# Local-head attention in units of 32 queries and 64 keys, with one transpose, copy and normalisation per 256 tokens

## The chip, the cores and the metric

One core of a Trainium2 chip. The time of a kernel is the device time of one execution in microseconds (us); several runs are made and their median is given. Beside it there is one profiled execution, from which every row below comes.

## The reference

Attention over 4 batches, 8 heads, 576 positions and 64 channels, then two feed-forward layers over the 2304 tokens with 512 channels. The first four heads look at the last 32 positions only, and these are the heads that the change touches:

```python
rel = pos[:, None] - pos[None, :]
mask_local = (rel >= 0) & (rel < 32)                      # heads 0 to 3
mask_strided = (rel >= 0) & (pos[None, :] % 32 == pos[:, None] % 32)   # heads 4 to 7
scores = np.where(masks, q @ k.T / sqrt(64), -1e9)
attn = exp(scores - max); attn = attn / (attn.sum(-1) + 1e-9)
x = attn @ v                      # -> (2304, 512)
h = x @ w_in; x = (h - tanh(h)) @ w_out                   # 512 -> 2048 -> 512
xn = x / rms(x) * rms_g
out = (silu(xn @ w_gate) * (xn @ w_val)) @ w_out2         # 512 -> 1536 -> 512
```

## The kernel before

The 2304 tokens are cut into nine subs of 256 tokens (`subs`): 0 to 3 are the first 256 positions of each batch, 4 is the last 64 positions of all four batches, 5 to 8 are positions 256 to 511. A sub has a `Local` object for heads 0 to 3 and, for heads 4 to 7, a `Dense` one (subs 0 to 3 and 6, on TensorE) or a `Strided` one (on GpSimd and VectorE). The subs form five groups, and while TensorE computes the first feed-forward layer of one group (`pe_h`, tiles ps_h; `pe_x`, tiles ps_x), the attention of the next group is put between. `Work` holds that attention as a list of stages, in the order local s, local p, dense s, local v, dense p, dense v; `run_pe` takes the next one at the steps that `STINT` names. From the second group on TensorE's order is the order in which the program is written. The order on the other engines is set by a scheduler at build time.

A stage of the local heads is one of three. **s** (`st_s`): 16 matmuls of a 64x64 block of q against 96 keys for the 256 queries, into two PSUM banks; then VectorE adds the mask and takes the maxima (`st_m`, one instruction per head and half), ScalarE takes the exponentials with their sums (`st_e`), VectorE divides (`st_n`, three instructions per half of 128 queries). **p** (`st_p`, `st_c`): per half four transposes and one copy of 96 partitions. **v** (`st_v`): 16 matmuls of a 96x64 block of v against 64 queries, then `st_y` (ScalarE) and `st_z` (VectorE) write the high and the low part into xs. `load_qk` and `load_v` of the next sub are issued behind s and v. The flag `fused` makes one p and one copy serve both halves; before, only `Dense` of subs 0 to 3 has it.

The attention of subs 0 and 1 has nothing to hide behind. Its order is written out as words in the string `START`, for all engines at once (`first` reads it): s, m, e, n, p, c, v, y, z as above, with the number of the sub, L (local) or D (dense) and the half; A, B, P, Q decode a weight tile in four steps (scale on ScalarE L170, merge on VectorE L176 and L177, high part on ScalarE L184, low part on VectorE L188); h, T, G, I, J, X are the pieces of the feed-forward units that come first (matmul into ps_h, tanh, subtract, high, low, matmul into ps_x). The line after `<` is the order of the loads, all on SyncE's queue. In subs 0 and 1 (`early`) the mask is added by TensorE (ps_s<-tab) and the maximum is a plain reduction. Matmuls all have line 147 (`mm`), transposes line 437.

Of the kernel before, what the change touches and what calls it, by code (L numbers as in the profile page):

```python
# [25 lines left out]
W9 s0Lx m0L0 e0L0 m0L1 s0Dx n0L0 e0L1 m0D0 p0L0m1 m0D1 s1Lx A0 e0D0 B0 c0L0a n0L1 p0L1h1 P0 Q0 m1L0 m1L1 e0D1 c0L1a  # L26
v0Lh0 s1Dx n0D1 n0D0 A1 e1L0 p0Dh1 e1L1 y0L1 n1L0 m1D0 m1D1 c0Da n1L1 v0Dm0m1 y0L0 e1D0 y0D1 z0L0 y0D0 z0L1 p1L0h1
c1L0a B1 z0D0 P1 z0D1 p1L1h1 e1D1 c1L1a Q1 n1D0 n1D1 h0h0 A2 v1Lm1 T0 B2 A3 G0 y1L0 p1Dh1 c1Da y1L1 B3 v1Dh1m0 I0 P2
J0 y1D1 z1L0 y1D0 h1h0 T1 z1L1 z1D1 z1D0 P3 h2h1 Q2 G1 A4 Q3 T2 B4 I1 G2 J1 I2 J2 X0
# [4 lines left out]
def attn_moe_moe_kernel(  # L34
# [3 lines left out]
    near_v: bass.AP,  # L38
# [4 lines left out]
    v_loc: bass.AP,  # L43
# [74 lines left out]
    tab = one.tile([128, 544], F32, name="tab")  # L118
    ident, mask, dmask = tab[:, 192:320], tab[:, 320:416], tab[:, 416:544]
    add = tab[:, 0:192].bitcast(BF16)  # L120
    ident16, add = add[:, 0:128], {96: add[:, 128:320].rearrange("q (u t) -> q u t", u=2), 64: add[:, 320:384]}
# [228 lines left out]
    class Heads:  # L350
        def __init__(self, j):
            self.j, self.near, self.early = j, j < NEAR, j < EA
            self.ps, self.sm, self.nm, self.ss, self.pp, self.pT, self.v = {}, {}, {}, {}, {}, {}, {}
            self.slot, self.both, self.sums = {}, None, None
            self.fused = False
# [9 lines left out]
        size = {"sm": 512, "pT": 512, "v": 512}  # L365

        def st_s(self, bank):
# [3 lines left out]
            for hh in range(2):  # L371
                if self.early:
                    m = add[w]
                    m = m.unsqueeze(2) if w == 96 else m.unsqueeze(1).unsqueeze(1)
# [12 lines left out]
        def st_m(self, i):  # L387
# [10 lines left out]
            self.ss[i] = att.tile([128, 2, 2], F32, tag="ss", name="ss", bufs=4)  # L398
            m = dmask if w == 128 else mask if not self.near else add[96][:, i] if w == 96 else add[64]
# [22 lines left out]
        def st_n(self, i):  # L422
            sm, ss = self.sm[i], self.ss.pop(i)
# [3 lines left out]
                out=sm, in0=sm, in1=ss.unsqueeze(3).to_broadcast([128, 2, 2, self.w]), op=ALU.mult  # L427
# [27 lines left out]
    class Local(Heads):  # L455
        w = 96

        def __init__(self, j):
            super().__init__(j)
            self.runs = runs(j)  # L460
            self.at, self.kw = [], 0
            if self.near:
                self.at, self.kw = [0, 32, 96, 160], SUB
            else:
                for _, _, n, _ in self.runs:
                    self.at += range(self.kw, self.kw + n, 64)
                    self.kw += W + n

        def load_qk(self):
# [6 lines left out]
            for b, t0, n, x0 in self.runs:  # L476
# [4 lines left out]
                o = self.at[x0 // 64]  # L481
                nc.sync.dma_start(out=self.kT[:, :, o:o + W + n], in_=k_loc[b, :, :, t0 - W:t0 + n])

        def load_v(self, i):
            if self.early:
                t = held.tile([128, 1024], F32, tag="v", name="v")[0:96]
                nc.sync.dma_start(out=t, in_=near_v[self.j])
                for i in range(2):
                    self.v[i] = t[:, 512 * i:512 * i + 512].rearrange("k (u f) -> k u f", u=2)
                return  # L490
            t = self.room("v", i, 512)[0:96]
            self.v[i] = t.rearrange("k (u f) -> k u f", u=2)
            if self.near:
                nc.sync.dma_start(out=t, in_=near_v[self.j, :, 512 * i:512 * i + 512])
                return
            at = [b * S + t - W for b, t in subs[self.j][2 * i:2 * i + 2]]
            first = v_loc[0, 0:96, :]
            (sp, _), (sf, nf) = first.ap
            nc.sync.dma_start(
                out=self.v[i],  # L500
                in_=bass.AP(
                    tensor=first.tensor, offset=v_loc.offset + at[0] * sp,
                    ap=[[sp, 96], [(at[1] - at[0]) * sp, 2], [sf, nf]],
                ),
            )

        def st_v(self, bank):
            ps = bank("ps_v").rearrange("r (i p u t) -> r i p u t", i=2, u=2, p=2)
            for i in range(2):
# [9 lines left out]
            self.po = {i: ps[:, i] for i in range(2)}  # L519
# [202 lines left out]
    class Work:  # L722
# [23 lines left out]
        def stage(o, nm):  # L746
            if nm == "s":
# [4 lines left out]
                for i in range(2):  # L752
# [10 lines left out]
            if nxt:  # L763
                if nm == "s":
                    nxt.load_qk()
                if nm == "v" and isinstance(o, Local):
                    for i in range(2):
# [671 lines left out]
```

## Time and profile before

| | |
|---|---|
| median of 3 runs | 889.43 us (888.55 to 890.35) |
| the profiled execution | 887.7 us |
| its span, first to last instruction | 885.9 us (so 1.8 us lie around it) |
| mean granted TensorE clock | 0.996 |
| TensorE (PE) busy | 868.8 us, 98% |
| VectorE (DVE) busy | 668.5 us, 75% |
| ScalarE (ACT) busy | 397.9 us, 45% |
| GpSimd (POOL) busy | 280.0 us, 32% |

Matmuls overlap in the array and the ends of the records are modelled, so the price of a group of matmuls is read from its start to the start of the group behind it. A float32 matmul leaves two records.

### The profile page before, as it was taken

The numbers are of one execution on the slowest core, as the hardware profiler recorded it, in microseconds if no ns is written. First come the engines' busy times: TensorE is split into PE (matmuls) and PEld (weight loads), VectorE is DVE, ScalarE is ACT, GpSimd is POOL, SyncE is SP. The second block draws the span as 40 slices with busy tenths as digits, with TensorE's granted clock in tenths as the row PEclk, the third lists the DMA queues.
The fourth block names the chain that finished last, engine by engine and source line by source line (L and its number), as shares of the span: only waits on it lengthen the run. The fifth ranks groups of instructions, "written<-read, shape, count | busy, mean of one in ns | idle before, by whom it ended". The sixth has DMA issues, their size and how long they took to land.

```text
span 885.9 us, 14105 instructions
## 1 busy us (share of the span) xinstructions
PE 868.8 (98%) x5091; PEld 739.7 (83%) x5091; DVE 668.5 (75%) x1376; ACT 397.9 (45%) x897; POOL 280.0 (32%) x315
## 2 busy tenths in 40 slices
PE   6999999999999999999999999999999999999998
PEld 4888888888998887888887888888878988888986
DVE  5999788888779887179978898576997953445444
ACT  6987643332544333265637553355332533422320
POOL 0000147695276952000000569676442400000000
PEclk8999999999999999999999999999999999999999
DMA  9955224311313000199828777799659139955002
GB/s 328 379 196 173 77 73 151 111 50 36 116 54 110 28 16 1 46 291 346 280 72 270 279 250 270 252 415 364 232 179 349 48 114 355 397 168 166 1 0 84
DMA packets 58566, 157.84 MB, mean 178 GB/s; under 512 B 9536, under 2 KB 20672, under 8 KB 58496
## 3 DMA queue, kind: packets, MB, share of 16 engines
q1 hardware_dynamic: 57344, 155.89, 50.0%
q10 hardware_dynamic: 1152, 1.05, 0.3%
q8 instruction: 40, 0.66, 0.3%
q14 instruction: 30, 0.25, 0.1%
HBM read 119.16 MB, written 37.75 MB: 177 GB/s over the span
## 4 chain that ended last, share of the span: by engine, by line
PE 82%; DVE 8%; POOL 5%; ACT 2%; issue 1%; DMA 1%; SPq 0%; DVEq 0%; POOLq 0%; ACTq 0%
PE ps_x L147 21%; PE ps_h L147 21%; PE ps_pr L147 18%; PE ps_o L147 12%; POOL pr L629 4%; PE ps_m L147 4%; PE ps_q L147 3%; DVE so L669 3%; DMA raw<-in_w_in_dram 1%; PE ps_s L147 1%; POOL pr L662 1%; PE ps_v L147 1%; ACT sm L416 1%; PE ps_p L437 1%; DVE x L957 0%
## 5 line engine op out<-in xcount | busy, mean ns | idle before, releaser
L147 PE MATMUL ps_h<-xs,w 128*128 128x512 f32 (+1 forms) x984 | 213.4, 365 | 0.7 <-DVE tg L814 0.7
L147 PE MATMUL ps_x<-g,w 128*128 128x512 f32 (+1 forms) x984 | 214.0, 366 | 0.0
L147 PEld LDWEIGHTS ps_h<-xs,w 128*128 128x128 f32 x984 | 169.0, 189 | 30.6 <-DVE tg L814 1.1
L147 PEld LDWEIGHTS ps_x<-g,w 128*128 128x128 f32 x984 | 168.6, 189 | 30.0 <-issue 0.2
L147 PE MATMUL ps_pr<-xt,wt 128*128 128x448 f32 x576 | 123.1, 366 | 2.2 <-DVE s L1040 1.4
L629 POOL TENSOR_TENSOR pr<-sk,sq 128x256 f32<-128x256 f32 (+2 forms) x101 | 82.5, 852 | 131.8 <-DMA sq<-in_q_str_dram 126.4
L147 PE MATMUL ps_o<-wt,p 128*128 128x512 f32 x504 | 120.2, 390 | 0.0
L147 PEld LDWEIGHTS ps_pr<-xt,wt 128*128 128x128 f32 x576 | 107.9, 188 | 13.5 <-DVE s L1040 2.2
L147 PEld LDWEIGHTS ps_o<-wt,p 128*128 128x128 f32 x504 | 94.6, 188 | 18.7
L820 ACT CAST g<-tg 128x512 fp32r<-128x512 f32 (+1 forms) x82 | 46.6, 568 | 108.9 <-DVE tg L814 108.8
L662 POOL TENSOR_TENSOR pr<-sv,se 128x288 f32<-128x288 f32 (+12 forms) x104 | 69.7, 691 | 56.7 <-DVE so L669 19.8
L1050 ACT COPY u<-ps_pr 128x448 f32<-128x448 f32 x72 | 38.2, 533 | 84.8 <-PE ps_pr L147 84.7
L814 DVE SCALAR_TENSOR_TENSOR tg<-ps_h,tg 128x512 f32<-128x512 f32 (+1 forms) x82 | 50.8, 619 | 28.0 <-ACT tg L809 28.0
L669 DVE TENSOR_REDUCE so<-pr 128x16 f32<-128x272 f32 (+11 forms) x104 | 65.0, 653 | 8.7 <-POOL pr L662 8.4
L971 POOL TENSOR_TENSOR tr<-x 128x896 f32<-128x896 f32 x4 | 15.1, 3765 | 171.1 <-DMA raw<-in_w_gate_dram 153.9
L809 ACT ACTIVATE tg<-ps_h 128x512 f32<-128x512 f32 (+1 forms) x82 | 44.2, 539 | 48.1 <-PE ps_h L147 48.1
L1101 DVE SCALAR_TENSOR_TENSOR osum<-ps_o,osum 128x512 f32<-128x512 f32 x70 | 47.9, 687 | 21.6 <-PE ps_o L147 20.9
L825 DVE TENSOR_TENSOR g<-tg,g 128x512 fp32r<-128x512 f32 (+1 forms) x82 | 55.3, 677 | 10.8 <-ACT g L820 10.2
L147 PE MATMUL ps_pr<-xt,wo 128*128 128x448 f32 x288 | 60.8, 366 | 0.2 <-ACT u L1050 0.2
L147 PEld LDWEIGHTS ps_pr<-xt,wo 128*128 128x128 f32 x288 | 54.0, 188 | 5.2 <-ACT u L1050 0.6
L184 ACT CAST w<-ct 128x512 fp32r<-128x512 f32 x68 | 42.1, 619 | 30.3 <-DVE ct L177 28.2
L634 DVE TENSOR_REDUCE sc<-pr 128x4 f32<-128x256 f32 (+2 forms) x101 | 43.8, 437 | 12.1 <-POOL pr L629 11.6
(110 smaller groups left out, 1201.4 us busy)
## 6 DMA issues: line engine op xcount, KB each, us to landing
wt<-w SPq DMA_DIRECT2D x84, 512.0 KB, 5.9
raw<-in_w_out_dram SPq DMA_DIRECT2D x28, 512.0 KB, 6.1
raw<-in_w_gate_dram SPq DMA_DIRECT2D x24, 512.0 KB, 5.9
raw<-in_w_val_dram SPq DMA_DIRECT2D x24, 512.0 KB, 6.8
w<-w SPq DMA_DIRECT2D x24, 512.0 KB, 6.6
w<-wo SPq DMA_DIRECT2D x24, 512.0 KB, 8.2
raw<-in_w_in_dram SPq DMA_DIRECT2D x16, 512.0 KB, 9.9
out_dram<-osum SPq DMA_DIRECT2D x18, 256.0 KB, 2.1
```

What stands on the lines that cost most here:

```text
L147: nc.tensor.matmul(out_, lhsT, rhs, start=start, stop=stop, skip_group_check=True)
L184: nc.scalar.copy(out=self.t[:, 0].rearrange("p c f -> p (c f)"), in_=self.b)
L629: nc.gpsimd.tensor_tensor(out=pr, in0=self.k[:, a:e, :], in1=self.q[:, c - c0:c - c0 + 1, :].to_broadcast([128, e - a, D]), op=ALU.mult,)
L634: pend.append(lambda: nc.vector.tensor_reduce(out=s[:, c - c0, a:e], in_=pr, axis=AX.X, op=ALU.add))
L662: nc.gpsimd.tensor_tensor(out=pr, in0=self.v[:, 0:c + 1, a:e], in1=self.e[:, c - c0, 0:c + 1].unsqueeze(2).to_broadcast([128, c + 1, e - a ...
L669: pend.append(lambda: nc.vector.tensor_reduce(out=o[:, c - g0, a:e], in_=pr.rearrange("l c d -> l d c"), axis=AX.X, op=ALU.add))
L809: nc.scalar.activation(out=t, in_=h_of[g, f, a], func=ACTF.Tanh, scale=WS)
L814: nc.vector.scalar_tensor_tensor(out=t, in0=h_of.pop((g, f, a)), scalar=WS, in1=t, op0=ALU.mult, op1=ALU.subtract)
L820: nc.scalar.copy(out=t[:, 0], in_=t_of[g, f, a])
L825: nc.vector.tensor_tensor(out=t[:, 1], in0=t_of.pop((g, f, a)), in1=t[:, 0].bitcast(F32), op=ALU.subtract)
L1050: nc.scalar.copy(out=u, in_=x[kd])
L1101: nc.vector.scalar_tensor_tensor(out=o, in0=ps, scalar=WS, in1=o, op0=ALU.mult, op1=ALU.add)
```

## The change

`Local` now works on units of 32 queries, each with the 64 keys that end with its own: its key offsets `at` are 32 apart, `w` is 64 and `fused` is on. So s has 32 matmuls of a 64x32 block of q against 64 keys; the probabilities of both halves lie side by side, 128 columns wide, and n, p and c are one each for 256 queries (p: four transposes of 128x128, c: a copy of 128 partitions). For v the 64 keys of the first half stand on partitions 0 to 63 and those of the second on 64 to 127: 32 matmuls of 64x64 against 32 queries, one half into one PSUM bank and the other into a second. v comes from a new input `v_win`, in which the windows lie ready as 128 rows of 1024 numbers for each sub (512 KB, in place of 96 rows, 384 KB), in one transfer where subs 2 to 8 had two. The mask table is 480 numbers wide instead of 544. `START` is a new list.

```diff
 START = """
 <tabcdwABwCDwww2ww
-W9 s0Lx m0L0 e0L0 m0L1 s0Dx n0L0 e0L1 m0D0 p0L0m1 m0D1 s1Lx A0 e0D0 B0 c0L0a n0L1 p0L1h1 P0 Q0 m1L0 m1L1 e0D1 c0L1a
+W9 s0Lx s0Dx m0L1 m0L0 e0L1 e0L0 m0D1 m0D0 e0D1 n0L p0Lm0 A0 s1Lx B0 e0D0 s1Dx c0La P0 m1L1 A1 v0Lh0h1 m1L0 e1L1 n0D
...
+            n = self.unit
             for i in range(2):
                 for p in range(2):
-                    for k in range(2):
+                    for x in range(0, 128, n):
                         for hh in range(2):
-                            r, u = slice(64 * hh, 64 * hh + 64), 2 * i + k
+                            r, t = slice(64 * hh, 64 * hh + 64), 128 * i + x
+                            a = self.at[t // n]
                             mm(
-                                ps[hh][64 * k:64 * k + 64, i, p, :], self.q[r, u, p, :],
-                                self.kT[r, p, self.at[u]:self.at[u] + w], not self.early, True,
+                                ps[hh][x:x + n, i, p, :], self.q[r, t // 64, p, t % 64:t % 64 + n],
+                                self.kT[r, p, a:a + w], not self.early, True,
                             )
...
     def st_n(self, i):
-            sm, ss = self.sm[i], self.ss.pop(i)
+            if self.fused:
+                sm = self.both.rearrange("q h p i t -> q (h p i) t")
+                ss = self.sums.rearrange("q h p i -> q (h p i)")
...
     class Local(Heads):
-        w = 96
+        w = 64
...
+            self.fused, self.local, self.unit = True, True, W
...
-        def load_v(self, i):
+        def load_v(self):
             if self.early:
...
+                t = held.tile([128, 1024], F32, tag="v", name="v")
+            else:
+                t = one.tile([128, 1024], F32, tag="v", name="v")
+            self.v = t.rearrange("k (c f) -> k c f", f=256)
+            nc.sync.dma_start(out=t, in_=v_win[self.j])
 
         def st_v(self, bank):
-            ps = bank("ps_v").rearrange("r (i p u t) -> r i p u t", i=2, u=2, p=2)
-            for i in range(2):
-                pT, v = self.pT.pop(i), self.v.pop(i)
-                for u in range(2):
-                    for p in range(2):
-                        for hh in range(2):
-                            h = 2 * p + hh
+            ps = [bank("ps_v")[:, :256].rearrange("r (p t) -> r p t", p=2) for _ in range(2)]
+            pT = self.pT.pop(0)
+            for c in range(4):
+                for p in range(2):
+                    for hh in range(2):
+                        for i in range(2):
+                            h, r, x = 2 * p + hh, slice(64 * i, 64 * i + 64), W * c
                             mm(
-                                ps[64 * hh:64 * hh + 64, i, p, u, :], v[:, u, 64 * h:64 * h + 64],
-                                pT[:, hh, p, 64 * u:64 * u + 64], True, True,
+                                ps[i][64 * hh:64 * hh + 64, p, x:x + W], self.v[r, c, 64 * h:64 * h + 64],
+                                pT[r, hh, p, x:x + W], True, True,
                             )
```

What that does to the order is seen at two places. The first is TensorE from the transposes of sub 1's local heads to the first ps_x of the feed-forward layer (v<-pT,v are the local values, pT,dv the dense ones, ps_h the feed-forward units, ps_s<-lq the scores of sub 2). Before:

```order
L437 MATMUL ps_p<-tab,sm 96x128 x8
L147 MATMUL ps_h<-xs,w 128x256 x12
L147 MATMUL ps_v<-pT,v 64x64 x16
L437 MATMUL ps_p<-tab,sm 128x128 x4
L147 MATMUL ps_v<-pT,dv 32x64 x32
L147 MATMUL ps_h<-xs,w 128x256 x12
L147 MATMUL ps_s<-lq 64x96 x13
L147 MATMUL ps_h<-xs,w 128x256 x12
L147 MATMUL ps_x<-g,w 128x256 x12
```

and now:

```order
L450 MATMUL ps_p<-tab,sm 128x128 x4
L146 MATMUL ps_h<-xs,w 128x256 x12
L146 MATMUL ps_v<-pT,v 64x32 x32
L450 MATMUL ps_p<-tab,sm 128x128 x4
L146 MATMUL ps_h<-xs,w 128x256 x12
L146 MATMUL ps_s<-lq 32x64 x8
L146 MATMUL ps_v<-pT,dv 32x64 x32
L146 MATMUL ps_x<-g,w 128x256 x12
L146 MATMUL ps_h<-xs,w 128x256 x6
```

The second ps_h unit has moved ahead of the dense values of sub 1, and the first ps_x ahead of the third ps_h unit. The second place is ScalarE, from the copy of sub 1's first local transposes to the copy that the dense values of sub 1 wait for (the last pT<-ps_p here; ca<-raw are scale steps, w<-ct casts of weight tiles). Before:

```order
L442 COPY pT<-ps_p 96x512
L184 CAST w<-ct 128x512
L416 ACTIVATE sm,ss<-ps_s,nm 128x64 x4
L442 COPY pT<-ps_p 96x512
L170 ACTIVATE ca<-raw 128x512
L809 ACTIVATE tg<-ps_h 128x256
L170 ACTIVATE ca<-raw 128x512
L445 CAST xs<-ps_v 128x2x128
L442 COPY pT<-ps_p 128x512
```

and now, from the exponentials of sub 1's dense heads on:

```order
L424 ACTIVATE sm,ss<-ps_s,nm 128x64 x8
L455 COPY pT<-ps_p 128x512
L183 CAST w<-ct 128x512
L805 ACTIVATE tg<-ps_h 128x256
L183 CAST w<-ct 128x512
L458 CAST xs<-ps_v 128x2x128 x2
L816 CAST g<-tg 128x256
L455 COPY pT<-ps_p 128x512
```

A second weight cast, a second evacuation and the cast of g now stand ahead of the last copy, where they stood behind it. Of the two scale steps one (`A2` in the words) has moved up, ahead of the first of these rows, and the other (`A3`) behind the last; one local copy is gone.

## Rows read from the trace of the kernel before

**Rows 1.** Page, part 1: busy time of each engine, share, instructions

```profile
PE 868.8 (98%) x5091; PEld 739.7 (83%) x5091; DVE 668.5 (75%) x1376; ACT 397.9 (45%) x897; POOL 280.0 (32%) x315
```

**Rows 2.** Page, part 4: chain that ended last, share by engine

```profile
PE 82%; DVE 8%; POOL 5%; ACT 2%; issue 1%; DMA 1%; SPq 0%; DVEq 0%; POOLq 0%; ACTq 0%
```

**Rows 3.** Waits of TensorE: who waited for whom, total us, times, longest

```profile
PE ps_v L147 <- ACT pT L442: 1.8, 2, 1.2
...
PE ps_h L147 <- DVE tg L814: 0.7, 1, 0.7
```

**Rows 4.** Busy time by stretch (PE, PEld, DVE, ACT, POOL, clock, DMA share, GB/s)

```profile
10.00:20.00 10.00, 7.79 (x112) 5.94 (x112) 7.98 (x29) 8.66 (x45) 0.00 (x0) 0.66 1.03 363
20.00:30.00 10.00, 6.92 (x191) 6.01 (x192) 9.48 (x29) 9.99 (x36) 0.00 (x0) 1.00 1.04 345
30.00:40.00 10.00, 10.00 (x91) 8.86 (x90) 10.00 (x33) 8.11 (x20) 0.00 (x0) 1.00 1.03 407
```

**Rows 5.** Timeline of TensorE, sub 4's local stages: start, us, instruction, records

```profile
147.50 0.89 PE L147 MATMUL ps_s<-lq 64*64 64x96 f32 x32
148.32 3.06 PE L147 MATMUL ps_x<-g,w 128*128 128x512 f32 x12
...
159.39 1.04 PE L437 MATMUL ps_p<-tab,sm 128*96 128x128 f32 x8
160.18 3.00 PE L147 MATMUL ps_x<-g,w 128*128 128x512 f32 x12
...
171.26 1.15 PE L147 MATMUL ps_v<-pT,v 96*64 96x64 f32 x32
172.35 3.02 PE L147 MATMUL ps_x<-g,w 128*128 128x512 f32 x12
```

**Rows 6.** Timeline of TensorE, sub 3's dense stages s, p and v

```profile
102.16 0.69 PE L147 MATMUL ps_s<-dq 64*64 64x64 f32 x32
102.78 3.92 PE L147 MATMUL ps_x<-g,w 128*128 128x512 f32 x16
...
114.66 0.60 PE L437 MATMUL ps_p<-tab,sm 128*128 128x128 f32 x4
115.01 2.77 PE L147 MATMUL ps_h<-xs,w 128*128 128x512 f32 x11
...
120.20 0.86 PE L147 MATMUL ps_v<-pT,dv 64*32 64x64 f32 x64
120.99 0.50 PE L147 MATMUL ps_x<-g,w 128*128 128x512 f32 x1
```

**Rows 7.** Timeline of TensorE around the end of START

```profile
28.29 0.86 PE L147 MATMUL ps_v<-pT,dv 64*32 64x64 f32 x64 [0.68 <-ACT pT L442]
29.07 1.69 PE L147 MATMUL ps_h<-xs,w 128*128 128x256 f32 x12
30.70 1.10 PE L147 MATMUL ps_s<-lq 64*64 64x96 f32 x26
...
34.70 2.91 PE L147 MATMUL ps_h<-xs,w 128*128 128x512 f32 x12
```

**Rows 8.** Timeline of ScalarE in START

```profile
16.93 0.67 ACT L170 ACTIVATE ca<-raw 128x512 f32<-128x512 f32 x1 [0.79 <-DMA raw<-in_w_in_dram]
...
25.41 0.58 ACT L442 COPY pT<-ps_p 96x512 f32<-96x512 f32 x1
...
27.65 0.59 ACT L442 COPY pT<-ps_p 128x512 f32<-128x512 f32 x1
...
28.39 0.42 ACT L820 CAST g<-tg 128x256 fp32r<-128x256 f32 x1
28.70 0.63 ACT L184 CAST w<-ct 128x512 fp32r<-128x512 f32 x1
```

**Rows 9.** Groups by line and shape, VectorE: count, busy us, mean ns, idle before

```profile
L426 DVE TENSOR_TENSOR sm<-sm,ss 128x384 f32<-128x384 f32 x18 | 10.8, 598 | 0.2
...
L426 DVE TENSOR_TENSOR sm<-sm,ss 128x512 f32<-128x512 f32 x2 | 1.5, 746 | 0.0
```

More of the change, by code (lines that the diff above doesn't have):

```diff
@@ L42, in attn_moe_moe_kernel @@
     k_loc: bass.AP,
-    v_loc: bass.AP,
+    v_win: bass.AP,
     q_str: bass.AP,
@@ L354, in __init__ @@
             self.slot, self.both, self.sums = {}, None, None
-            self.fused = False
+            self.fused, self.local, self.unit = False, False, 64
         def room(self, name, i, words):
@@ L397, in st_m @@
             self.nm[i] = nm = att.tile([128, 2, 2], F32, tag="nm", name="nm", bufs=4)
-            self.ss[i] = att.tile([128, 2, 2], F32, tag="ss", name="ss", bufs=4)
-            m = dmask if w == 128 else mask if not self.near else add[96][:, i] if w == 96 else add[64]
+            if not self.fused:
+                self.ss[i] = att.tile([128, 2, 2], F32, tag="ss", name="ss", bufs=4)
+            else:
+                if self.sums is None:
+                    self.sums = att.tile([128, 2, 2, 2], F32, tag="ss", name="ss", bufs=4)
+                self.ss[i] = self.sums[:, :, :, i]
+            if self.local:
+                m = add_l[:, i] if self.near else mask
+            else:
+                m = add_d if self.near else dmask
             for hh in range(2):
@@ L426, in st_n @@
             nc.vector.tensor_tensor(
-                out=sm, in0=sm, in1=ss.unsqueeze(3).to_broadcast([128, 2, 2, self.w]), op=ALU.mult
+                out=sm, in0=sm, in1=ss.unsqueeze(2).to_broadcast(list(sm.shape)), op=ALU.mult
             )
@@ L480, in load_qk @@
                 )
-                o = self.at[x0 // 64]
+                o = self.at[x0 // W]
                 nc.sync.dma_start(out=self.kT[:, :, o:o + W + n], in_=k_loc[b, :, :, t0 - W:t0 + n])
-        def load_v(self, i):
+        def load_v(self):
             if self.early:
-                t = held.tile([128, 1024], F32, tag="v", name="v")[0:96]
-                nc.sync.dma_start(out=t, in_=near_v[self.j])
-                for i in range(2):
[L489 to L505, printed above, removed]
@@ L518, in st_v @@
                             )
-            self.po = {i: ps[:, i] for i in range(2)}
+            self.po = {i: ps[i].rearrange("r p (u t) -> r p u t", t=64) for i in range(2)}
         def dst(self, i):
@@ L751, in stage @@
                     o.st_e(i)
-                for i in range(2):
+                for i in range(1 if o.fused else 2):
                     o.st_n(i)
@@ L765, in stage @@
                     nxt.load_qk()
-                if nm == "v" and isinstance(o, Local):
-                    for i in range(2):
-                        nxt.load_v(i)
-                elif nm == "v":
+                if nm == "v":
                     nxt.load_v()
@@ L1375, in values @@
         return residues(v, n).transpose(0, 5, 3, 4, 1, 2, 6).reshape(B, 8 * n, 4, 4 * D)
-    row, col = _np.arange(128)[:, None], _np.arange(96)[None, :]
-    r2 = row % 64
-    rel = r2 + 32 - col
-    near = (rel >= 0) & (rel < 32)
-    first = _np.where(row < 64, (r2 >= col) & (r2 - col < 32), near)
-    c2 = _np.arange(64)[None, :]
+    row, c2 = _np.arange(128)[:, None], _np.arange(64)[None, :]
+    r1, r2 = row % 32, row % 64
+    near = (r1 + 32 >= c2) & (r1 < c2)
+    first = _np.where(row < 32, row >= c2, near)
     same = (r2 // 8 == c2 // 8) & (c2 <= r2)
@@ L1403, in lay_out, with windows @@
     v_l = v[:, :4].transpose(0, 2, 1, 3).reshape(B, S, 4 * D)
+    subs = [[(b, t + 64 * u) for u in range(4)] for t in (0, 256) for b in range(B)]
+    subs[B:B] = [[(b, 512) for b in range(B)]]
+    def windows(sub):
+        r = [v_l[b, max(0, t + x - 32):][:64] for b, t in sub for x in (0, 32)]
+        return _np.stack(r).reshape(2, 4, 64, 4 * D).transpose(0, 2, 1, 3).reshape(128, 1024)
     q_d = residues(q, 16).reshape(B, 2, 2, 2, 8, 4, 8, D).transpose(0, 3, 2, 7, 5, 1, 6, 4).reshape(B, 2, 128, 512)
@@ L1406, in lay_out @@
         near_l=flat(q_l[:, :, :8], k_l[:, :, :, :256]),
-        near_v=flat(*(v_l[:, a:a + 96] for a in (0, 32, 96, 160))),
         near_d=flat(q_d[:, 0], keys(8)), v_near=values(8).reshape(B, 64, 2, 2, 256).transpose(0, 2, 1, 3, 4).reshape(B, 128, 512),
-        q_loc=q_l, k_loc=k_l, v_loc=v_l,
+        q_loc=q_l, k_loc=k_l, v_win=_np.stack([windows(s) for s in subs]),
         q_str=lanes(q), k_str=lanes(k), v_str=lanes(v),
```

36 lines of the change are left out of this document (18 added, 18 removed).

## The prediction

> **What bounds the kernel now.** I read the page's busy times first: TensorE works 868.8 of 885.9 us, and no other engine over 75% [rows 1]. The chain of waits says the same from the other end: 82% of what ended last is TensorE [rows 2]. So a microsecond of TensorE time taken out of the dense part is a microsecond of the kernel, as long as nobody else becomes late, and work of VectorE or ScalarE counts only where TensorE stands. The waits say where that is: 1.8 us for the copy pT in front of the values, and once 0.7 us for VectorE's tg in front of a ps_h unit [rows 3]. The stretches show the first kind in START: from 20 to 30 us TensorE is busy 6.92 of 10 while ScalarE is at 9.99, and from 30 us on TensorE is full [rows 4]. In the stretch before, the granted clock is 0.66, a mixture of its two levels, 1.2 and 2.4 GHz, after TensorE had stood still between short bursts; it is back at 1.00 from 20 us on. There are therefore two terms: the price of the local stages on TensorE in subs 2 to 8, which lie in the dense part, and the length of ScalarE's queue in START, which holds subs 0 and 1.
>
> **The local stages of subs 2 to 8.** The price is taken from the start of a stage to the start of the matmuls behind it. Sub 4: scores 148.32 - 147.50 = 0.82 us, transposes 160.18 - 159.39 = 0.79, values 172.35 - 171.26 = 1.09, together 2.70 us [rows 5]. The other six subs repeat this to within 0.1.
>
> Scores now: 32 matmuls of a 64x32 block against 64 columns. The same shape is in the trace, as the dense values of sub 3: 32 matmuls (64 records) in 120.99 - 120.20 = 0.79 us [rows 6], 24.6 ns each. The old ones cost 51 ns each (0.82 / 16). So twice the count is paid by eight tiles of the array at work where there were four, and by 64 columns in place of 96: 0.79, a gain of 0.03.
>
> Transposes now: four of 128x128, as in the dense stage: 115.01 - 114.66 = 0.35 [rows 6]. A gain of 0.44.
>
> Values now: 32 matmuls of a 64x64 block against 32 columns. No row has that. The two rows with 64x64 blocks are 16 matmuls against 64 columns, 102.78 - 102.16 = 0.62 [rows 6], and against 96 columns, 0.82 [rows 5]; the line through them gives 0.42 at 32 columns, so 0.84 for 32 matmuls. The bounds: 0.79 below, the cheapest matmul of the trace, and 1.24 above, if a matmul against 32 columns costs as much as one against 64 (32 x 38.8 ns). I take 0.84, since the line rests on the same blocks and the cheapest matmul lies right beside it. A gain of 0.25, with bounds of a gain of 0.30 and a loss of 0.15.
>
> Against that stands a rule of the Trainium skill (TensorEngine Tiling (Array Packing), Instruction Overhead): each matmul carries about 60 cycles, so that one column costs as much as 60, and a tiling factor is not to be taken from a dimension that is small already. By it the values would be at the upper bound, 1.24, and the sum below 2.8 us smaller. The trace speaks half for it: the price per column between 64 and 96 is straight, but no row lies under 64 columns. It has a chance of its own among the rivals.
>
> Sum: 2.70 - (0.79 + 0.35 + 0.84) = 0.72 us for a sub, times seven = 5.0 us (bounds 2.2 and 5.4). All of it lies in the dense part and nothing hides it. The values now need two PSUM banks at once where one did, but the stage ahead of them always lies several feed-forward units back, so its banks are free.
>
> **VectorE's relief.** A sub has one division where it had two: 2 x 598 - 746 = 450 ns less [rows 9], and shorter maxima. That counts only where VectorE is the late one, at the 0.7 us wait for tg [rows 3]; VectorE's relief and TensorE's earlier arrival are of one size there, so I take 0.3 us of the 0.7 (bounds: a loss of 0.7, if TensorE gains on it, and a gain of 0.7).
>
> **START.** What ends it is ScalarE's queue: from the second weight tile's scale step at 16.93, which had waited 0.79 us for its transfer, to the copy that ends at 27.65 + 0.59 = 28.24 [rows 8], with hardly a gap (9.99 of 10 busy [rows 4]). TensorE then starts the dense values of sub 1 at 28.29 and never stands again: 6.41 us of work up to 34.70 [rows 7].
>
> In the new order that queue starts later. The v window ahead of that weight tile is 128 KB larger, at 363 GB/s [rows 4] 0.36 us; the table is 32 KB smaller, 0.09 us. So 0.27 us later: the queues are full (share 1.03) and no slack is left to take it. Between the same marks the queue loses a local copy (0.58) and a scale step (0.67), and gets a weight cast (0.63), a cast of g (0.42) and an evacuation (not in the rows as such; I take it as the cast of g, 0.42): 0.22 us longer [rows 8]. The eight exponentials that shrink from 96 to 64 columns I leave out, as a small gain. The last copy ends at 28.24 + 0.27 + 0.22, and the dense values start at about 28.8.
>
> But now the second ps_h unit, 30.70 - 29.07 = 1.63 us [rows 7], stands ahead of them and can use TensorE's gap. If it is wholly hidden, the point that was reached at 34.70 is reached at 28.8 + 6.41 - 1.63 = 33.6, a gain of 1.1; if not at all, at 35.2, a loss of 0.5. It waits for the low part of its weight tile, which VectorE (9.48 of 10 busy) makes late, and behind START the first ps_x units wait for their low parts on the same queue. I take a gain of 0.4. The bounds are a gain of 2.0 (the 1.1, and half of the 1.8 us for pT [rows 3] besides) and a loss of 1.2: nothing hidden, and two more windows of 0.36 us each that hold up the weight tiles behind them.
>
> The load orders and counts on SyncE change little else: one transfer of v where there were two, 512 KB for 384. Beyond START I cost that at nothing: a window is asked for a whole sub ahead, and between two stages lie several units of 3 us [rows 5]. Uncovered it would be 0.36 us a sub.
>
> **Sum.** 5.0 + 0.3 + 0.4 = 5.7 us less. Against the profiled execution, 887.7 us with its span of 885.9, that is 882.0. The median of the runs is 889.43, 1.7 above that execution; 889.43 - 5.7 = 883.7 us.
>
> **Rivals.**
>
> The floor: a matmul against 32 columns costs as one against 64. Values 1.24, 0.32 us gained by a sub, 2.2 in all: 889.43 - 2.2 - 0.7 = 886.5 us. For it: no row lies under 64 columns. Against it: in rows 5 and 6 the price falls with the columns, and matmuls on smaller blocks come at 24.6 ns, so that nothing in the issue holds them at 38.8. Chance 0.13.
>
> START loses: the larger windows make the weights late, and the low parts on VectorE, full from 30 us on, hold TensorE: the bound above, a loss of 1.2 in place of the gain of 0.4: 883.7 + 1.6 = 885.3 us. For it: DMA share 1.03 and VectorE 10.00 [rows 4]. Against it: VectorE has less to do by two divisions a sub there. Chance 0.10.
>
> The gain is held up: in groups four and five VectorE and GpSimd do the strided heads, and the 0.7 us wait shows that they are just in time. If TensorE only waits longer there, the gains of subs 7 and 8 and half of those of 5 and 6 go, 3 x 0.72 = 2.2: 885.9 us. Against it: VectorE is relieved by the same subs. Chance 0.08.
>
> Slower: the price belongs to the instruction and not to its columns or blocks. Then 32 score matmuls cost 51 ns each, 1.64 us, and 32 value matmuls 68 ns each (1.09 / 16), 2.18; with 0.35 that is 4.17, 1.47 more than now, 10.3 for seven subs: 889.43 + 10.3 - 0.7 = 899.0 us. It decides from a mean of (2.70 - 0.35) / 64 = 36.7 ns a matmul. For it: the dense scores cost 38.8. Against it: the very shape of the new scores costs 24.6. Chance 0.06.
>
> **The numbers.** My forecast has 0.63, its own range is 881 to 885.5. Less than 0.2% (1.8 us) can hardly be told from no change here. The forecast, START and most of the two other cases lie below 887.6: faster 0.87; no change 0.06; slower 0.07, the last rival and a little for a cause not thought of. The range, with the bounds of START and of the wait below (883.7 - 1.6 - 0.4 - 0.4 for the values' lower bound = 881.3) and the floor above with a loss in START (886.5 + 1.6), is 881 to 888.
>
> **What would show it.** From the start of a local stage to the matmuls behind it: scores 0.79, transposes 0.35, values 0.84; values at 1.24 show the floor, both over 1.2 the last rival. In START the dense values of sub 1 start near 28.8 with ps_h ahead of them, and the wait for pT is shorter; the 512-wide ps_h unit of 34.70 comes later in the new order, so the sum of TensorE's waits up to 40 us is to be compared. I am wrong if TensorE's waits between 200 and 340 us grow to over 2 us, or if it waits for weights between 30 and 70 us.

## The result and the profile after

The changed kernel takes 895.19 us in the median of 19 runs (891.64 to 900.84), the kernel before 889.72 us beside it (19 runs): the ratio is 1.0063, 95% interval 1.0046 to 1.0080. The forecast was 883.7 us, with a range from 881 to 888; the time lies outside it, on the slower side. The profiled execution took 893.56 us with a span of 891.8, 5.9 more than the span before, and this is the difference to be found in the rows.

First the busy times (part 1 of the page of the changed kernel), the answer to [rows 1]:

```profile
PE 869.2 (97%) x5631; PEld 739.3 (83%) x5631; DVE 664.2 (74%) x1337; ACT 391.1 (44%) x888; POOL 281.0 (32%) x315
```

TensorE is as long at work as before and has 540 records more; VectorE and ScalarE have less to do, as the change intends. So the added time is, on balance, time in which TensorE stands still. TensorE's waits, the answer to [rows 3] (who waited for whom, total us, times, longest):

```profile
PE ps_h L146 <- DVE tg L810: 5.3, 4, 2.7
PE ps_p L450 <- ACT sm L424: 3.0, 1, 3.0
PE ps_p L450 <- DVE xs L462: 1.9, 1, 1.9
```

The wait for VectorE's tg was 0.7 us, once; now it is 5.3. Where it is, the timeline of TensorE shows, from sub 8's scores to its transposes, first of the changed kernel and then of the kernel before (start us, us, instruction, records, in brackets the idle time before it and who ended it):

```profile
318.92 0.86 PE L146 MATMUL ps_s<-lq 64*32 64x64 f32 x64
...
323.28 3.02 PE L146 MATMUL ps_h<-xs,w 128*128 128x512 f32 x12 [0.55 <-DVE tg L810]
...
330.66 3.03 PE L146 MATMUL ps_h<-xs,w 128*128 128x512 f32 x12 [1.64 <-DVE tg L810]
...
339.14 4.50 PE L146 MATMUL ps_h<-xs,w 128*128 128x512 f32 x12 [2.69 <-DVE tg L810]
343.48 0.60 PE L450 MATMUL ps_p<-tab,sm 128*128 128x128 f32 x4
```

```profile
319.97 0.89 PE L147 MATMUL ps_s<-lq 64*64 64x96 f32 x32
...
335.45 3.05 PE L147 MATMUL ps_h<-xs,w 128*128 128x512 f32 x12 [0.72 <-DVE tg L814]
338.34 1.04 PE L437 MATMUL ps_p<-tab,sm 128*96 128x128 f32 x8
```

The changed kernel comes to sub 8 1.05 us ahead (318.92 against 319.97) and leaves its transposes 5.14 us behind: 24.56 us for what took 18.37. Of the 6.19 us, 4.16 are waits (0.55 + 1.64 + 2.69 - 0.72) and 1.45 the last unit, 4.50 us where it was 3.05: the granted clock was 0.67 in 339 to 344 us, after TensorE had stood still for 2.69 us (busy 1.45 of 4.00 in 335 to 339):

```profile
335.00:339.00 4.00, 1.45 (x7) 0.86 (x5) 3.86 (x9) 0.30 (x1) 2.32 (x5) 0.99 0.00 0
339.00:344.00 5.00, 4.86 (x17) 3.93 (x18) 4.60 (x11) 1.03 (x3) 3.10 (x5) 0.67 0.04 2
```

The lower clock belongs to this execution. In the run with START's wait filled (below), which has the same orders here, a wait of 2.71 us is followed by a unit of 3.06 at clock 1.00, and sub 8 takes 23.30 us in place of 24.56; so 4.9 us of the loss are there without it.

The local stages themselves got cheaper. Sub 4 in the timeline, the answer to [rows 5]:

```profile
147.39 0.89 PE L146 MATMUL ps_s<-lq 64*32 64x64 f32 x64
148.21 0.96 PE L146 MATMUL ps_x<-g,w 128*128 128x512 f32 x3
...
159.22 0.60 PE L450 MATMUL ps_p<-tab,sm 128*128 128x128 f32 x4
159.58 1.18 PE L146 MATMUL ps_x<-g,w 128*128 128x512 f32 x4
...
170.68 1.13 PE L146 MATMUL ps_v<-pT,v 64*64 64x32 f32 x64
171.75 0.97 PE L146 MATMUL ps_x<-g,w 128*128 128x512 f32 x3
```

Scores 0.82, transposes 0.36, values 1.07: 2.25 us in place of 2.70 (in other subs the scores take 0.79). The whole account against the kernel before, by these marks: up to sub 4's scores -0.11, from there to sub 8's scores -0.94, from those to sub 8's values (354.94 against 350.22) +5.77, and behind them +1.18; together the 5.9. Of the last 1.18, 0.85 is one wait for VectorE's s (L1027) at 583 us that the kernel before does not have.

### What holds tg up

tg is an instruction of VectorE, and its place in VectorE's queue is fixed when the kernel is built. In the build of the changed kernel more reductions of the strided heads (so<-pr, L668) stand ahead of it: 84, 91 and 98 ahead of the three tg in question, where the kernel before has 83, 89 and 95. VectorE's timeline of the changed kernel between two of them (some rows left out):

```profile
329.92 0.69 DVE L810 SCALAR_TENSOR_TENSOR tg<-ps_h,tg 128x512 f32<-128x512 f32 x1
330.52 0.71 DVE L668 TENSOR_REDUCE so<-pr 128x21 f32<-128x273 f32 x1
...
336.36 0.73 DVE L668 TENSOR_REDUCE so<-pr 128x22 f32<-128x308 f32 x1
...
337.47 1.02 DVE L668 TENSOR_REDUCE so<-pr 128x16 f32<-128x240 f32 x2
338.41 0.67 DVE L810 SCALAR_TENSOR_TENSOR tg<-ps_h,tg 128x512 f32<-128x512 f32 x1
```

From tg to tg are 8.5 us, and 7.35 between the two before it, while a ps_h and a ps_x unit on TensorE together take 5.44 where nothing waits (324.37 to 329.81 in the run with SyncE in code order from group four on, below). Each so needs a product of GpSimd's first, and one reduction takes 0.5 to 0.7 us. The three tg of the kernel before:

```profile
320.06 0.68 DVE L814 SCALAR_TENSOR_TENSOR tg<-ps_h,tg 128x512 f32<-128x512 f32 x1
...
325.61 0.68 DVE L814 SCALAR_TENSOR_TENSOR tg<-ps_h,tg 128x512 f32<-128x512 f32 x1
...
334.71 0.68 DVE L814 SCALAR_TENSOR_TENSOR tg<-ps_h,tg 128x512 f32<-128x512 f32 x1
```

Its spacing is as wide, 5.55 and 9.10 us, but it starts ahead: its first tg ends 2.95 us before TensorE needs it (320.74 against 323.69), and TensorE waits only for the third. In the changed kernel the first of the three stands at 322.57, 2.51 us later, and from the first to the third pass 15.84 us in place of 14.65. So most of the delay is there at the first tg already, where only one reduction more stands ahead; the two more that come behind it, at 0.5 to 0.7 us each, are about the other 1.2 us.

The order on SyncE came out otherwise as well: sub 7's strided values sv are asked for behind sub 8's keys and queries. The rows of SyncE's queue and of GpSimd, before and after:

```profile
265.68 0.35 SPq L610 DMA_DIRECT2D sv<-in_v_str_dram  x1
267.83 0.35 SPq L604 DMA_DIRECT2D sk<-in_k_str_dram  x1
...
271.43 2.86 POOL L662 TENSOR_TENSOR pr<-sv,se 128x288 f32<-128x288 f32 x4 [3.63 <-DVE se L652]
```

```profile
266.58 0.33 SPq L603 DMA_DIRECT2D sk<-in_k_str_dram  x1
...
267.48 0.38 SPq L609 DMA_DIRECT2D sv<-in_v_str_dram  x1
272.74 2.67 POOL L661 TENSOR_TENSOR pr<-sv,se 128x288 f32<-128x288 f32 x4 [6.18 <-DMA sv<-in_v_str_dram]
```

GpSimd waits for that load now, and starts 1.3 us later. So there is theory A: the build's new order on SyncE (A1, the late load) or on VectorE (A2, the reductions ahead of tg) made the loss. Rival B: START and its clock. Rival C: the new operations cost more wherever they stand.

### The profile page after: what moved, and what is told of

Read it like the earlier page. It is cut to its first block, busy times and chain, and to the rows that moved or that the text cites. A ratio compares the mean times of both kernels' runs of the same rounds, so it can differ in the third digit from the quotient of the medians.

```text
span 891.8 us, 15109 instructions
## 1 busy us (share of the span) xinstructions
PE 869.2 (97%) x5631; PEld 739.3 (83%) x5631; DVE 664.2 (74%) x1337; ACT 391.1 (44%) x888; POOL 281.0 (32%) x315
## 3 DMA queue, kind: packets, MB, share of 16 engines
q10 hardware_dynamic: 1152, 1.05, 0.3%
## 4 chain that ended last, share of the span: by engine, by line
PE 61%; DVE 9%; POOL 4%; DMA 2%; issue 2%; SPq 0%; ACT 0%; POOLq 0%; DVEq 0%; ACTq 0%
PE ps_pr L146 18%; PE ps_o L146 12%; PE ps_x L146 12%; PE ps_h L146 12%; DVE so L668 4%; PE ps_m L146 4%; POOL pr L628 4%; PE ps_q L146 3%; DMA raw<-in_w_val_dram 1%; DVE g L821 1%; DVE tg L810 1%; POOL pr L661 1%; DMA sv<-in_v_str_dram 1%; DVE x L953 0%; DMA sq<-in_q_str_dram 0%
## 5 line engine op out<-in xcount | busy, mean ns | idle before, releaser
L146 PE MATMUL ps_h<-xs,w 128*128 128x512 f32 (+1 forms) x984 | 215.9, 368 | 5.3 <-DVE tg L810 5.3
L146 PEld LDWEIGHTS ps_h<-xs,w 128*128 128x128 f32 x984 | 171.5, 192 | 36.9 <-DVE tg L810 7.4
L668 DVE TENSOR_REDUCE so<-pr 128x16 f32<-128x272 f32 (+11 forms) x104 | 65.1, 652 | 9.5 <-POOL pr L661 8.7
```

The source lines that it names most:

```text
L146: nc.tensor.matmul(out_, lhsT, rhs, start=start, stop=stop, skip_group_check=True)
L668: pend.append(lambda: nc.vector.tensor_reduce(out=o[:, c - g0, a:e], in_=pr.rearrange("l c d -> l d c"), axis=AX.X, op=ALU.add))
```

## The experiments

Each ran beside the kernel before, and a ratio is to that. Its median was 887.82 us beside the one edge, the late load, the code order from group two on and the filled wait; 888.89 beside the code order from group four on, the new list and the value shapes; 890.15 beside the other three.

### One edge on SyncE: sub 8's sk and sq behind sub 7's sv

```diff
-                if self.nxt:
+                if self.nxt and self.nxt.j == 8:
+                    with tc.issue_after(self.sv.ins):
+                        self.nxt.load_qk()
+                elif self.nxt:
                     self.nxt.load_qk()
```

> The changed kernel with one edge: sub 8's loads of sk and sq stand behind sub 7's load of sv on SyncE, as in the kernel before. VectorE's order comes out with more strided reductions ahead of the three tg (87, 94, 102 against 84, 91, 98). Theory A1 (the late load decides): the waits for tg at sub 8 go, 889 to 891. Theory A2 (the number of reductions ahead of tg decides): the waits stay as long or grow, 895 to 899. Rivals B and C: 895.

893.93 us, ratio 1.0059 (1.0040 to 1.0078). GpSimd starts sub 7's products at 269.48, in good time, and TensorE waits all the same:

```profile
322.67 3.02 PE L146 MATMUL ps_h<-xs,w 128*128 128x512 f32 x12 [0.37 <-DVE tg L813]
329.74 3.06 PE L146 MATMUL ps_h<-xs,w 128*128 128x512 f32 x12 [1.34 <-DVE tg L813]
338.30 3.06 PE L146 MATMUL ps_h<-xs,w 128*128 128x512 f32 x12 [2.79 <-DVE tg L813]
```

The median lies between the two expectations (the profile is of its fastest execution, 890.17). With the load early again and VectorE's order not, sub 8 takes 22.71 us from scores to transposes; the 1.45 us of the low clock are gone in this run (3.06 for the last unit, behind a wait of 2.79), the waits are not. That speaks for A2, though they are no longer than in the changed kernel, with three or four reductions more ahead.

### The kernel before with the late load

```diff
                 if self.nxt:
                     self.nxt.load_qk()
+                if self.j == 7:
+                    with tc.issue_after(self.nxt.sq.ins):
+                        self.load_v()
```

(and sub 6's stage no longer asks for it.)

> The kernel before with the load of sub 7's sv put behind sub 8's sk and sq on SyncE, as the changed kernel has it; reductions ahead of the three tg are 81, 88, 95 (before 83, 89, 95). Theory A1 (the late load decides): 3 to 5 us slower than the kernel before, 892 to 895, with waits for tg of over 1.5 us at sub 8. Theory A2: within 1 us of the kernel before, 889 to 890.5. Rivals B and C: no difference, 889.5.

891.80 us, ratio 1.0042 (1.0020 to 1.0064), with no part of the change in it. VectorE's order is nearly that of the kernel before (81, 88, 95), and the late load makes one wait:

```profile
338.53 3.03 PE L147 MATMUL ps_h<-xs,w 128*128 128x512 f32 x12 [2.93 <-DVE tg L817]
```

Sub 8 takes 20.78 us, 2.4 more than before. So the late load costs time by itself too, a little less than expected, and without more reductions ahead of tg.

### SyncE in the order of the code, from group two on and from group four on

```diff
             if g == 1:
                 queue0.close()
                 order = ctx.enter_context(ExitStack())
-                order.enter_context(tc.manual_schedule(engines={mybir.EngineType.PE}))
+                order.enter_context(tc.manual_schedule(engines={mybir.EngineType.PE, mybir.EngineType.SP}))
```

> The changed kernel with SyncE's queue in the order of the code from group two on; by this VectorE's order in group five comes back too (strided reductions ahead of the three disputed tg: 82, 89, 95; kernel before 83, 89, 95; changed kernel 84, 91, 98). Theory A (the re-built orders on SyncE and VectorE in 265 to 340 us made the loss): TensorE's waits for tg around sub 8 fall from 0.55, 1.64 and 2.69 us to under 1 us each, and the time falls by 4 to 6 us to 889 to 891, ratio to the kernel before 0.999 to 1.002. Rival B (START and its clock): 894 to 895. Rival C (the new operations cost more wherever they stand): 894 to 896.

899.31 us, ratio 1.0127 (1.0091 to 1.0164), against the expectation. At sub 8 it did what theory A said: no wait for tg, 17.25 us from scores (331.79) to transposes (349.04). But the order of the code moves other loads as well, and from sub 5's transposes to sub 7's scores 85.08 us pass where the kernel before needs 75.10, with waits for tg of 1.90 and 2.56 us; which load makes these was not traced. So the same edit for the last groups only:

```diff
+            if g == 3:
+                order.enter_context(tc.manual_schedule(engines={mybir.EngineType.SP}))
             if g == NG - 1:
                 order.close()
```

> The changed kernel with SyncE's queue in the order of the code from group four on only (sub 7's sv ahead of sub 8's sk and sq); nothing ahead of that moves. VectorE then has 82, 89 and 95 strided reductions ahead of the three disputed tg, as the kernel before (83, 89, 95). Theory A (late load and reductions ahead of tg made the loss): from sub 8's scores to its transposes 17.2 us, as in the run with the whole queue in code order, instead of 24.6; sub 8's values start at 347 to 348.5, about 2 us ahead of the kernel before (350.22), and the time is 885 to 888.5, ratio to the kernel before 0.996 to 1.000. Rivals B (START) and C (the new operations' own cost): the time stays at 893 or more.

889.67 us, ratio 1.0012 (0.9991 to 1.0034): 4.5 us of the 5.6 are back, as theory A has it, and the two kernels' intervals do not meet (1.0046 and up for the changed kernel). TensorE's timeline at sub 8:

```profile
320.69 0.86 PE L146 MATMUL ps_s<-lq 64*32 64x64 f32 x64
...
335.25 2.89 PE L146 MATMUL ps_h<-xs,w 128*128 128x512 f32 x12
337.97 0.60 PE L450 MATMUL ps_p<-tab,sm 128*128 128x128 f32 x4
```

17.28 us (17.2 was expected), and no wait for tg in the list of TensorE's waits. Only the order on SyncE was set; VectorE's 82, 89, 95 follow from it in the build, so the run mends A1 and A2 together. B and C alone, which expected 893 or more, are out. The time misses the expected 885 to 888.5 us by over 1 us. Sub 4's scores start at 149.38, 1.88 behind the profile of the kernel before; from there to sub 8's values 2.47 us are gained.

The kernel before with the same edit is the control:

> The kernel before with SyncE's queue in code order from group four on; VectorE's order in group five stays (83, 89, 95 reductions ahead of the three tg). Theory A: the kernel before already had sub 7's sv in time, so 0 to 1 us faster at most (ratio 0.998 to 1.001), the one wait of 0.72 us for tg may go. If the order by itself were worth the 4 to 5 us, it would be 884 to 885.

890.41 us, ratio 1.0005 (0.9988 to 1.0023); the order by itself is worth nothing there, and one wait of 0.61 us for tg is left. Its START is that of the kernel before, and yet sub 4's scores start at 150.13 in its profile, 2.63 later than there and 0.75 later than in the run above: the clock was 0.50 from 10 to 25 us, where the profile of the kernel before has 0.76, 0.56 and 1.00. So START differs by over 2 us between executions of one and the same program order, and the 1.88 us above show no loss by the change.

### START: filling the wait, and another list

```diff
-... z0L0 p1Lm1 z0L1 h0h0 ...
+... z0L0 F8 p1Lm1 z0L1 h0h0 ...
```

> The changed kernel with eight matmuls of the identity on an unused bank in START, behind the values of D0 and ahead of p1L, where TensorE waits 1.9 us; results unchanged. SyncE's order and VectorE's in group five are those of the changed kernel. Rival B (the clock lost in START is what is missing): the first ps_h takes 1.67 instead of 2.77 us, sub 4's scores start about 1.3 us earlier and the time falls by over 3 us to under 892. Theory A: the gain of about 1.3 us in START is seen at sub 4, the waits at sub 8 stay, and the time is 893.5 to 895.

895.33 us, ratio 1.0065 (1.0042 to 1.0087): no gain. In the profiled execution START was even longer (sub 4 at 151.07), with the clock at 0.50 from 10 to 25 us already ahead of the filling matmuls at 22.68. At that clock the eight matmuls took 2.99 us, more than the wait that they were to fill, and the edit also moved TensorE's order in the rest of group one. So the run decides nothing on B. It shows a wait that the changed kernel's own profile has not: 1.69 us, named issue (nothing in the profile ends it), inside the values of L0.

```diff
-c0Da A2 m1D1 v0Dm0m1 m1D0 n1L y0L1 y0L0 B2 y0D0 y0D1 e1D0 z0D0 z0D1 e1D1 z0L0 p1Lm1 z0L1 h0h0 c1La B1 ... v1Lm0m1
+c0Da m1D1 v0Dm0m1 m1D0 n1L p1Lx y0L1 y0L0 A2 z0L1 z0L0 y0D0 y0D1 z0D0 z0D1 c1La h0h0 e1D0 e1D1 v1Lm0m1 B2 B1 ...
```

> The same, and START's list changed: the transposes of L1 go to a free bank straight behind the values of D0, z0L and z0D ahead of the second weight's conversion on VectorE, the copy of L1 ahead of D1's exponentials on ScalarE, and the first ps_h ahead of L1's values. Rival B (START still costs): TensorE's wait of 1.9 us ahead of L1's transposes goes, the first ps_h starts 0.8 us earlier and does not run at half the clock, sub 4's scores start 1 to 2.5 us earlier and the time falls by as much below the run without it. Theory A alone: the same time within 1 us, since the time up to sub 8 is then lost in waiting.

890.57 us, ratio 1.0023 (1.0003 to 1.0044), beside 1.0012 without the new list. The first ps_h starts 0.93 us earlier (23.55 against 24.48), but still takes 2.65 us, and sub 4's scores start no earlier (149.34 against 149.38). Rearranging this wait gained nothing.

### START: is it the code?

The timeline of TensorE in the run with SyncE's late groups set, around the wait named issue:

```profile
15.43 0.47 PE L146 MATMUL ps_v<-pT,v 64*64 64x32 f32 x9
17.32 1.71 PE L146 MATMUL ps_v<-pT,v 64*64 64x32 f32 x55 [1.43 <-issue]
```

In four of the seven profiled kernels with the new stages it is there, always after exactly 222 records; in the run with the one edge on SyncE it comes after 475, and in the control (the kernel before with SyncE's late groups set) after 221, at 22.10 us, and lasts 0.30. Part 3 of the page, the queue of TensorE's code, before and after (packets, MB, share):

```profile
q8 instruction: 40, 0.66, 0.3%
```

```profile
q8 instruction: 44, 0.72, 0.3%
```

2 x 5091 instructions in 40 packets and 2 x 5631 in 44 are 255 and 256 for a packet of 16.4 KB, so 128 records (64 float32 matmuls) with their weight loads, and 222, 350 and 478 are one packet apart; a trace can lack a few records. Theory D: the new stages use up the code sooner, when the DMA rings are full (share 1.03 [rows 4]), and the next packet is late. The Trainium skill (Runtime: NRT & Kernel Launch, Instruction fetch mechanics) has the packet of 256 instructions, which the trace bears out, and says that the cost of crossing from one to the next is mostly hidden, which START shows otherwise.

The transfers of this queue in the traces show the wait to be one for code. In the run above a packet starts at 14.9 us and TensorE goes on at 17.32. The other waits named here, too, end 2.4 to 2.7 us after the start of a packet. In the changed kernel's own profile the same packet starts at 10.6, and TensorE passes the place without a wait. Up to there the two executions agree (the values of L0 start at 15.43 and 15.35); behind it the run above is 1.8 us late, and at sub 4 1.99. Why the packet moves 4 us later in some executions is open: the DMA share from 5 to 10 us is 0.91 to 1.02 in those without the wait at 222 and 0.94 to 1.02 in those with it, so that full rings make it late is argued and not shown.

Two runs, one that shortens the code and one that lengthens it:

```diff
-            n = self.unit
+            n = 64 if self.early else self.unit
...
-            for c in range(4):
+            n = 64 if self.early else W
+            for c in range(0, 4, n // W):
```

> The run with SyncE's queue in code order from group four on, and the local scores and values of subs 0 and 1 (those of START) in 32 matmuls of 64 queries instead of 64 of 32 (so the odd units of these two subs see the even units' window: another output). TensorE's code for START is as short as in the kernel before. Theory D (in START TensorE runs out of code: pages of 256 matmuls with their weights come over the loaded DMA rings): no wait named issue inside the values of L0 or within 256 matmuls behind it, sub 4's scores start at 146 to 147.5 instead of 149.38, and the time is 1.5 to 3 us under the run without it, 886 to 888.5, ratio to the kernel before 0.996 to 0.999. Rival E (the waits for the softmax of L0 and for D0's remainders decide): 889 to 890, sub 4 at 148.5 or later.

888.40 us, ratio 0.9989 (0.9969 to 1.0010), 0.0023 below the run without it, though the two intervals overlap; no wait named issue, and sub 4's scores start at 146.79, 2.59 us earlier. A packet is 64 float32 matmuls by the counts above, not the 256 of the expectation. The packet in question starts at 15.9 here, but TensorE comes to its 222nd record only inside the values of D0, which start at 18.43. Against the changed kernel's own profile, which has twice these matmuls and no such wait either, sub 4 is 0.60 us earlier. And of the 2.59 us 0.80 is left at sub 8's values (348.83 against 349.63), with four waits for tg between, 1.7 us in all.

```diff
+                            n = 48 if self.early and w == 96 else w
+                            for x in range(0, w, n):
...
+                            n = 32 if self.early else 64
+                            for x in range(0, 64, n):
```

> The kernel before with the local scores of subs 0 and 1 in 64 matmuls of 48 keys instead of 32 of 96 and their values in 64 of 32 queries instead of 32 of 64: the results are the same, TensorE's code for START is as long as in the changed kernel. Theory D: a wait named issue of 1 to 2 us appears in START, and the time is 1 to 3 us over the kernel before, ratio 1.001 to 1.004. Rival E: only the matmuls' own price, 0.3 to 0.8 us.

893.30 us, ratio 1.0044 (1.0023 to 1.0065): the kernel before, with nothing changed but the number of matmuls in subs 0 and 1, loses nearly as much as the change as a whole, a little more than expected. The wait comes at record 222 and again at 349:

```profile
15.48 1.50 PE L147 MATMUL ps_v<-pT,v 96*64 96x32 f32 x39
17.75 0.92 PE L147 MATMUL ps_v<-pT,v 96*64 96x32 f32 x25 [0.78 <-issue]
...
24.08 0.64 PE L439 MATMUL ps_p<-tab,sm 128*96 128x128 f32 x4 [2.34 <-issue]
```

Sub 4's scores start at 151.67, 4.17 behind the kernel before. The waits for code take the place of others: up to the second ps_h unit (33.01 against 29.07 [rows 7]) all of TensorE's waits together are 9.9 us, against 8.7 before. So about 1.2 of these 3.94 us are waits, and 2.8 are longer work: more matmuls (sub 0's scores take 1.18 us in place of 0.82) and a lower clock (0.66 from 25 to 30 us, where the first ps_h unit takes 2.62 us in place of 1.60 and sub 1's values 2.48 in place of 1.22). So the place and the cause of the wait are as D has them, in both directions. That the wait makes up the loss of this run is not shown: E was right that the matmuls have a price of their own, though 0.3 to 0.8 us was too low.

### What a value matmul costs

```diff
+            n = {4: 16, 6: 64}.get(self.j, W)
+            d = 32 if self.j == 7 else 64
...
+                for x in range(W * c, W * c + W, n):
+                    if x % n:
+                        continue
+                    for y in range(0, 64, d):
```

(and sub 5 with hh ahead of i in the order.)

> The changed kernel with the local values in another shape in each sub: sub 4 with 16 columns a matmul (128 of them), sub 5 with 32 columns and the head halves innermost in the order, sub 6 with 64 columns (32 matmuls; queries of the second unit are multiplied with the first's window, so the output is another), sub 7 with 32 weight columns (128 of them), sub 8 as it is. Theory V1 (a 64x64 block has a floor that 32 columns do not go below): 33 ns at 16 columns (a slot of 4.2 us), 1.07 us at sub 5, 38 ns at 64 columns (1.2 us), and with 32 weight columns about 25 ns (3.1 us). Rival V2 (the order of the row halves costs): sub 5 takes 0.84 us. Rival V3 (the price goes with the columns): 16 columns at 28 ns or less (under 3.6 us).

The expectation counted records as matmuls: a matmul here has two records, so its slots are twice too long; its times for one matmul stand. From the start of the values to the matmul behind them, subs 4, 5, 6 and 7:

```profile
170.85 2.12 PE L146 MATMUL ps_v<-pT,v 64*64 64x16 f32 x128
172.90 0.50 PE L146 MATMUL ps_x<-g,w 128*128 128x512 f32 x1
...
230.60 1.14 PE L146 MATMUL ps_v<-pT,v 64*64 64x32 f32 x64
231.67 1.58 PE L146 MATMUL ps_h<-xs,w 128*128 128x256 f32 x11
...
256.34 0.69 PE L146 MATMUL ps_v<-pT,v 64*64 64x64 f32 x32
256.96 0.50 PE L146 MATMUL ps_x<-g,w 128*128 128x256 f32 x2
...
312.56 1.29 PE L146 MATMUL ps_v<-pT,v 64*32 64x32 f32 x128
313.77 1.19 PE L146 MATMUL ps_x<-g,w 128*128 128x512 f32 x4
```

A 64x64 block costs 2.05 / 64 = 32.0 ns against 16 columns, 1.07 / 32 = 33.4 against 32 in either order, 0.62 / 16 = 38.8 against 64; a 64x32 block against 32 columns 1.21 / 64 = 18.9. V1 holds: from 64 to 32 columns the price falls by 14%, from 32 to 16 hardly. V2 and V3 are out. (One execution, 898.15 us; its time has more in it than these slots, a wait of 4.30 us for tg ahead of sub 5 among it, and is not used.)

## Why the prediction was wrong

**The step that failed is the one that cost the order at nothing.** The prediction let the gains of the dense part stand unless VectorE was already late, and said of SyncE that "the load orders and counts on SyncE change little else" and "beyond START I cost that at nothing". The build moved one load of the strided heads and put one to three more reductions ahead of three tg. That costs 6.2 us between sub 8's scores and its transposes (4.9 in an execution without the low clock), where a gain of 0.3 had been forecast (0.03 for the scores, and VectorE's relief). It is shown by setting SyncE's order: the 24.56 us become 17.28 and the ratio 1.0012, while the kernel before gains nothing by the same edit.

**The rival for it was there, but bounded wrongly.** "The gain is held up" had the place and the engines, and "I am wrong if TensorE's waits between 200 and 340 us grow to over 2 us" is what happened (5.3 us). Its price was the loss of the gains, 2.2 us, and its end a time still faster than before. A queue that is just in time can do more than swallow a gain: the kernel before lived on the 2.95 us by which its first tg was ahead, and 2.5 us of delay used them up, since VectorE takes 15.8 us (14.7 before) for the two pairs of units that TensorE does in 10.9. The rival also set VectorE's relief against it, and the new order cost more than the relief gave.

**START was taken as a gain of 0.4, and no profile shows one.** In the changed kernel's own profile sub 4's scores are 0.11 us early; two subs' gains of 0.49 lie ahead of them, so START lost 0.9, with no wait named issue. In the run with SyncE's late groups set the loss is 2.9 us against the profile of the kernel before, but 0.2 against the control's. The bound was a loss of 1.2, and the size stays open, since one START alone differs by 2.6 us between executions. The queue of ScalarE, on which the term rested, was forecast well: the dense values of sub 1 start at 28.34 in the changed kernel's profile, against 28.8 forecast. The clock, on which the term had nothing, was lower: from 20 to 30 us TensorE was busy 8.33 of 10 us, but at clock 0.83 where [rows 4] has 1.00. TensorE's own code was not on the list either.

**The values were mis-sized.** 0.84 was read off a line through 64 and 96 columns, and two points cannot show that the price goes on straight below them; measured are 1.07, within the bounds. The step gains 0.49 in place of 0.72 for a sub, 3.4 in place of 5.0 for seven. The rule of the Trainium skill (TensorEngine Tiling (Array Packing), Instruction Overhead), that few columns cost as much as 60, comes nearer than the line: 33.4 ns against 38.8 at 64 columns and 32.0 at 16.

**Right were** the scores (0.79 to 0.82), the transposes (0.35), the fall of VectorE's and ScalarE's work, and against the last rival that the price is not one for every matmul. With the order mended, from sub 4's scores to sub 8's values 2.47 us are gained, of which 0.72 is the wait of [rows 3]; 1.75 is left of five times 0.49, and the difference of 0.7 is not traced.

**What stays open.** How the 6.2 us divide between the load and the reductions: the load alone cost 2.4 in the kernel before, the reductions alone 4.3 (22.71 - 18.37) in the changed kernel with the load early, where they are 87, 94 and 102, and no run has VectorE's old order with the late load in the changed kernel. What the change does to START in the median is open too: the profiles differ by what the code packet and the clock did in one execution, and the medians of the two kernels with SyncE's late groups set (1.0012 and 1.0005) do not show the gain of the dense part. Behind sub 8 the spans differ by 1.2 us (536.86 against 535.68 before); the same part took 541.3 in the kernel before with the late load and 535.7 with the one edge on SyncE, so it does not go with the change alone. Of the 1.2, 0.85 is the wait for s at 583 us, which the run with the one edge does not have; why it comes was not looked for. No version beat the kernel before: with the order set and START's code shortened (with another output) the ratio is 0.9989, and its interval holds 1.

## What to carry to other kernels

Where the build orders the queues, an edit to one engine's work is an edit to all of them: before costing the rest at nothing, count what stands ahead of each instruction that the bounding engine waits for, before and after, multiply by its duration, and look at which loads have changed places; here three more reductions, 1.5 to 2.1 us, are less than half of the 4.75 us by which the third tg came later after sub 8's scores. An engine that is just in time can turn a gain into a loss larger than the gain. And matmuls that are cheap one by one still have to be fetched: in this start-up the code for twice the matmuls came too late in some executions. One profile of a start-up is not enough to price it.

## What was not expected of the hardware

TensorE's code comes in packets of 16.4 KB, 128 matmul records with their weight loads, and in START it stood 0.8 to 2.3 us at their borders (records 222 and 349, once 475), until 2.4 to 2.7 us after the start of the packet's transfer. A 64x64 block costs 32.0, 33.4, 38.8 ns at 16, 32, 64 columns, a 64x32 block 18.9 ns at 32. A standstill of 2.69 us was followed by a unit of 4.50 us in place of 3.05, at a granted clock of 0.67, and one of 2.86 us (the run of the value shapes) by a unit of 5.49; but standstills of 2.71, 2.79 and 2.93 us in three other runs were followed by units of 3.03 to 3.06 at clock 1.00.
